# Linear attention and two expert layers on one core: scores masked on VectorE, scans one step earlier, state scaled on ScalarE, weight narrowing spread over three stages, sums of the second routing on TensorE

## The chip, the cores and the metric

The kernel runs on one core of a Trainium2 chip. Its engines are TensorE (PE; its weight loads are PEld), VectorE (DVE), ScalarE (ACT), GpSimd (POOL) and SyncE (SP, which here only issues transfers). Each engine works through its own instructions in order. The metric is the device time of one execution in microseconds; the kernel before takes 875.71 us (median of three runs, 875.18 to 875.74).

## The reference

Three parts follow one another. The first is linear attention with a decay, over 4 batches, 8 heads, 768 positions and a head size of 48. The second gives each of the 3072 tokens to one of 8 experts with room for 384 tokens each, in the order of the logits. The third is a dense layer with a squared ReLU.

```python
for t in range(S):
    state = alpha[:, :, t, :, None] * state + einsum('bhd,bhe->bhde', k[:, :, t], v[:, :, t])
    y[:, :, t] = einsum('bhd,bhde->bhe', q[:, :, t], state)
...
for idx in argsort(-logits.flatten()):
    tok, e = idx // E, idx % E
    if assigned[tok] >= 0 or counts[e] >= cap: continue
    assigned[tok] = e; counts[e] += 1
...
out[mask] = maximum(x[mask] @ w1[e], 0) @ w2[e]
...
g = maximum(x @ w_in, 0) ** 2
return g @ w_out
```

The two matrices of the last layer (384 x 2048 and 2048 x 384) come as 64-bit floats. The kernel reads their words as pairs of 32-bit integers and makes float32 of them ("narrowing"), kept as a high and a low half of 12 bits each.

## The kernel before

**Order.** The program order of each engine is the order in which the code is written; no scheduler moves anything. What is called first in the loop stands first in each engine's queue, and an instruction that waits holds up all behind it on its engine.

**Attention.** 24 chunks of 128 positions, 6 per batch, are the steps s = 0 to 23 of the main loop; two chunks are a unit (u = s // 2, c = s % 2). For each unit `prep` scales q and k: a VectorE scan over the alphas from behind (`f_t`, L144), GpSimd's product of k with it (L146), a reciprocal (L148), a copy of the ends (`be`, L149), a scan from ahead (`b_t`, L150) and the product of q with it (L152). `prep(u + 2)` runs a part at a time: the first scan at c = 1 of unit u, the second later in that step, the product of q at c = 0 of the next unit. In a step, `state_mm` (L231) makes the chunk's k v product, which VectorE adds to the state and multiplies by the decay (L239, L240); `scores` (L212) makes the scores of the next chunk, ScalarE copies them out of PSUM (L215) and GpSimd clears what lies above the diagonal (L216); `state_bd` (L248) copies the state into a block-diagonal tile; `k_tok` (L222) transposes k; `x_out` (L276 to L279) transposes the chunk before and writes it to DRAM (`x_d`); `y_mm` adds the part from the state (L256, full 128 x 128 products) and the part from the scores (L263); `logits` and `logits_t` make the router's logits, four chunks at a time.

**Narrowing.** `narrow` takes two pieces of 256 columns in every step: three VectorE instructions on each (L179, L182, L185), ScalarE's copy of the high half (L172) and GpSimd's difference (L173). The 48 raw pieces pass through four buffers; `narrow_load` issues the next transfer from SP as one comes free. All pieces are done about when the loop ends.

**First routing.** Six rounds find the threshold: products that count (L420), VectorE's test (`cg`), a product with a matrix of ones, VectorE's next digits, with warming products (L358) between. Then come the places, the chosen tokens' rows (L623, gathered by GpSimd) and the first expert's weights (`w_load0`, L798 and L799: high half on ScalarE, low half on VectorE).

**Experts.** For each of the 8 experts 8 steps of `gemm1` and `gemm2` and 16 of `gemm3` and `gemm4` run on TensorE. `tick` puts the next expert's routing between the products, a piece at a time: in each of 8 rounds `cross` issues two products (L428), three VectorE instructions (L433, L436, L437) and a GpSimd sum over all partitions (L440). VectorE reads that sum some products later.

Of the kernel before, what the change touches and what calls it, by code (L numbers as in the profile page):

```python
# [28 lines left out]
E = 8  # L29
# [13 lines left out]
NWP = 256  # L43
NWB = 4
BIG = 1.5e38
WD = 3
S0 = NS - 7
# [6 lines left out]
def kernel(ctx, tc, q, k, al, v, wg, w1, w2, w_in, w_out, out):  # L54
# [15 lines left out]
    wih = consts.tile([128, KD, F2], FR)  # L70
    wil = consts.tile([128, KD, F2], FR)
    woh = consts.tile([128, NF2, DM], FR)
    wol = consts.tile([128, NF2, DM], FR)

# [20 lines left out]
    def load(u, ends=(CU * HP,)):  # L95
        """q, k and alpha of a unit, whole or in parts of so many pairs"""
        i = u % NSL
        n0 = 0
        for n1 in ends:
            for t, src in ((as_[i], al), (ks[i].rearrange("p c a s -> p (c a s)"), k),  # L100
                           (qs[i].rearrange("p c a s -> p (c a s)"), q)):
# [15 lines left out]
    load(0, (2, 4, 8))  # L117
    load_v(0)
    bd = [ap_.tile([128, HP, 128], FT, name=f"bd{i}") for i in range(2)]
    nc.gpsimd.memset(bd[0], 0.0)  # L120
    nc.gpsimd.memset(bd[1], 0.0)
# [10 lines left out]
    def prep(u, n0=0, n1=CU * HP):  # L132
        """scaled q and k of one unit; yields after each VectorE scan"""
# [13 lines left out]
        yield  # L147
        nc.vector.reciprocal(d_b[:, cs, 0], f_t[:, cs, 0])  # L148
        nc.vector.tensor_copy(bend[i].rearrange("p c a -> p (c a)")[:, cs], f_t[:, cs, 0])  # L149
# [5 lines left out]
    wq = []  # L155
    for h_, l_, src in ((wih, wil, w_in), (woh, wol, w_out)):
        h2, l2, s2 = (t.rearrange("p a b -> p (a b)") for t in (h_, l_, src))
        wq += [(h2[:, j:j + NWP], l2[:, j:j + NWP], s2[:, j:j + NWP]) for j in range(0, h2.shape[1], NWP)]
    raws = []

    def narrow_load():
        if len(raws) < len(wq):
            raw = aw.tile([128, NWP, 2], U32, name="raw", bufs=NWB)
            nc.sync.dma_start(raw.rearrange("p a b -> p (a b)"), wq[len(raws)][2].bitcast(U32))
            raws.append(raw)

    def narrow():
        """float64 words -> float32 bits, kept as two halves of 12 bits each"""
        prev = []
        for i in range(0, len(wq) + 2, 2):  # L170
            for t, dst_h, dst_l in prev:
                nc.scalar.activation(dst_h, t.bitcast(FT), AF.Copy)  # L172
                nc.gpsimd.tensor_tensor(dst_l, t.bitcast(FT), dst_h.bitcast(FT), op=OP.subtract)  # L173
            prev = []
            if i < len(wq):
                js = (i, i + 1)
                ts = [aw.tile([128, NWP], U32, name=f"nb{j - i}") for j in js]
                for t, j in zip(ts, js):
                    nc.vector.tensor_scalar(t, raws[j][:, :, 1], 3, 0x3FFFFFF8, op0=OP.logical_shift_left,  # L179
                                            op1=OP.bitwise_and)  # L180
                for t, j in zip(ts, js):
                    nc.vector.scalar_tensor_tensor(t, raws[j][:, :, 1], 0xC0000000, t, op0=OP.bitwise_and,  # L182
                                                   op1=OP.bitwise_or)
# [531 lines left out]
    for _ in nw:  # L715
        pass
# [369 lines left out]
```

## Time and profile before

| what | value |
|---|---|
| median of three runs | 875.71 us |
| span of the profiled execution | 874.0 us |
| TensorE busy | 811.1 us (93%) |
| VectorE busy | 558.7 us (64%) |
| ScalarE busy | 398.1 us (46%) |
| GpSimd busy | 256.1 us (29%) |
| mean granted TensorE clock | 0.946 |
| chain that ended last | TensorE 69%, VectorE 16%, issue 10% |

The shares are means over stages with different limits. The attention lasts until about 192 us, the first routing until about 239 us, and the experts fill the rest. Rows of the timeline give the start and the length of an instruction, or of several alike (x8, say), whose lengths overlap a little; the distance between starts is what one takes of its engine.

### The profile page before, as it was taken

How to read it: one execution, taken by the hardware profiler on the slowest of the kernel's cores; microseconds unless marked ns; L12 is line 12 of the kernel's file. 1: busy time of each engine (PE TensorE's matmuls, PEld its weight loads, DVE VectorE, ACT ScalarE, POOL GpSimd, SP SyncE). 2: the span in 40 equal slices, each digit the busy share in tenths (PEclk: the TensorE clock that was granted, in tenths of full speed). 3: DMA queues.
4: the chain of work that ended last, by engine and by line, in shares of the span. 5: the costliest groups of instructions: out<-in, count | busy, mean ns of one | idle time of the engine just before them, and what ended most of it. 6: DMA issues, size and time to landing. Idle time of an engine off the chain costs nothing.

```text
span 874.0 us, 15157 instructions
## 1 busy us (share of the span) xinstructions
PE 811.1 (93%) x5592; PEld 764.8 (87%) x5592; DVE 558.7 (64%) x1528; ACT 398.1 (46%) x904; POOL 256.1 (29%) x248
## 2 busy tenths in 40 slices
PE   4876878789899999999999999999999999999996
PEld 3755767677599999999999999999999999999996
DVE  8999999983576577567656665765666542432211
ACT  3544546451234553464346245534634553662443
POOL 6687887960111131112201221220131210101001
PEclk9988787895799999999999999999999999999998
DMA  8557768521310230131023004201400332210000
GB/s 302 163 149 203 205 189 214 159 79 55 121 61 1 71 111 20 38 101 62 1 73 100 29 1 136 64 1 55 109 37 1 92 104 59 82 37 28 1 1 28
DMA packets 30219, 73.01 MB, mean 84 GB/s; under 512 B 4384, under 2 KB 8224, under 8 KB 30144
## 3 DMA queue, kind: packets, MB, share of 16 engines
q1 hardware_dynamic: 23616, 57.88, 23.2%
q0 software_dynamic: 3072, 9.44, 3.2%
q10 hardware_dynamic: 3456, 4.72, 1.6%
q8 instruction: 44, 0.72, 0.3%
q14 instruction: 31, 0.25, 0.1%
HBM read 62.58 MB, written 9.44 MB: 82 GB/s over the span
## 4 chain that ended last, share of the span: by engine, by line
PE 69%; DVE 16%; issue 10%; POOL 3%; DMA 2%; SPq 0%; ACT 0%; DVEq 0%; POOLq 0%; ACTq 0%
PE hu_p L842 10%; PE hu_p L844 10%; PE hu_p L843 10%; PE acc L926 7%; PE acc L927 7%; PE acc L922 7%; PE acc L842 3%; PE acc L844 3%; PE acc L843 3%; DVE nb L179 3%; DVE nb L182 3%; DVE nb L185 2%; DVE b_t L150 2%; DVE f_t L144 2%; PE rt_p L420 2%
## 5 line engine op out<-in xcount | busy, mean ns | idle before, releaser
L913 DVE TENSOR_TENSOR gl<-rg,gh 128x384 fp32r<-128x384 f32 x127 | 72.2, 568 | 165.5 <-ACT rg L912 164.7
L910 ACT ACTIVATE rg<-hu_p 128x384 f32<-128x384 f32 x128 | 63.0, 492 | 171.5 <-PE hu_p L844 168.1
L842 PE MATMUL hu_p<-zh,wih 128*128 128x384 f32 x384 | 131.5, 342 | 0.0
L926 PE MATMUL acc<-woh,gh 128*128 128x384 f32 x381 | 130.6, 343 | 0.0
L844 PE MATMUL hu_p<-zl,wih 128*128 128x384 f32 x384 | 129.9, 338 | 0.0
L843 PE MATMUL hu_p<-zh,wil 128*128 128x384 f32 x384 | 128.8, 335 | 0.0
L927 PE MATMUL acc<-wol,gh 128*128 128x384 f32 x381 | 128.6, 338 | 0.0
L440 POOL PARTITION_ALL_REDUCE tot<-ex x48 | 52.3, 1089 | 258.3 <-DVE ex L437 258.3
L922 PE MATMUL acc<-woh,gl 128*128 128x384 f32 x381 | 125.8, 337 | 0.0
L877 ACT ACTIVATE hh<-hu_p 128x384 fp32r<-128x384 f32 x64 | 31.5, 492 | 138.7 <-PE hu_p L844 138.7
L878 DVE SCALAR_TENSOR_TENSOR hl<-hu_p,hh 128x384 fp32r<-128x384 f32 x64 | 35.6, 556 | 63.9 <-ACT hh L877 63.8
L844 PEld LDWEIGHTS hu_p<-zl,wih 128*128 128x128 f32 x384 | 72.1, 188 | 1.2
L843 PEld LDWEIGHTS hu_p<-zh,wil 128*128 128x128 f32 x384 | 72.2, 188 | 0.0
L842 PEld LDWEIGHTS hu_p<-zh,wih 128*128 128x128 f32 x384 | 72.1, 188 | 0.0
L926 PEld LDWEIGHTS acc<-woh,gh 128*128 128x128 f32 x381 | 71.5, 188 | 0.1
L927 PEld LDWEIGHTS acc<-wol,gh 128*128 128x128 f32 x381 | 71.6, 188 | 0.0
L922 PEld LDWEIGHTS acc<-woh,gl 128*128 128x128 f32 x381 | 71.2, 188 | 0.0
L623 POOL DMA_INDIRECT xg<-x_d,ix x24 | 26.4, 1102 | 151.7 <-DVE pe L639 94.2
L911 ACT ACTIVATE gh<-rg 128x384 fp32r<-128x384 f32 x127 | 66.7, 525 | 4.0
L842 PE MATMUL hu_p<-xh,w1h 128*128 128x384 f32 x192 | 66.3, 345 | 0.0
L844 PE MATMUL hu_p<-xl,w1h 128*128 128x384 f32 x192 | 65.7, 342 | 0.0
L948 POOL DMA_INDIRECT out_dram<-ob,ix x24 | 23.7, 988 | 143.0 <-DVE ob L946 139.5
(252 smaller groups left out, 1885.6 us busy)
## 6 DMA issues: line engine op xcount, KB each, us to landing
wraw<-in_w_dram SPq DMA_DIRECT2D x62, 384.0 KB, 3.3
raw<-in_w_in_dram SPq DMA_DIRECT2D x24, 256.0 KB, 3.2
raw<-in_w_out_dram SPq DMA_DIRECT2D x24, 256.0 KB, 3.6
vt<-in_v_dram SPq DMA_DIRECT2D x12, 384.0 KB, 5.4
x_d<-xo ACTq DMA_DIRECT2D x24, 192.0 KB, 2.8
a<-in_al_dram SPq DMA_DIRECT2D x18, 193.7 KB, 4.7
k<-in_k_dram SPq DMA_DIRECT2D x18, 192.0 KB, 5.5
q<-in_q_dram SPq DMA_DIRECT2D x18, 192.0 KB, 6.1
```

The lines of the kernel that those rows point to most:

```text
L440: nc.gpsimd.partition_all_reduce(tot[:, :, :J], ex[:, :, :J], 128, bass_isa.ReduceOp.add)
L842: nc.tensor.matmul(dst, wh, xh, start=first, stop=False)
L843: nc.tensor.matmul(dst, wl, xh, start=False, stop=False)
L844: nc.tensor.matmul(dst, wh, xl, start=False, stop=last)
L877: nc.scalar.activation(hh, hp, AF.Relu)
L878: nc.vector.scalar_tensor_tensor(hl, hp, 0.0, hh.bitcast(FT), op0=OP.max, op1=OP.subtract)
L910: nc.scalar.activation(r, up, AF.Relu)
L911: nc.scalar.activation(gh, r, AF.Square)
L913: nc.vector.tensor_tensor(gl, g, gh.bitcast(FT), op=OP.subtract)
L922: nc.tensor.matmul(acc[j], gl[:, j * 128:(j + 1) * 128], woh[:, f, :], start=False, stop=(f == NF2 - 1))
L926: nc.tensor.matmul(acc[j], gh[:, cs], woh[:, f, :], start=(f == 0), stop=False)
L927: nc.tensor.matmul(acc[j], gh[:, cs], wol[:, f, :], start=False, stop=False)
```

## The change

- **Masking.** The scores go from PSUM to SBUF by one VectorE instruction for each half, a bitwise AND with a mask of ones and zeros. ScalarE's copies and GpSimd's clearing are gone.
- **State.** VectorE still adds; the decay is four ScalarE instructions with a scale per partition. The block-diagonal tile is gone: the part of y from the state is eight products of 48 x 48 blocks in place of four of 128 x 128, into two PSUM tiles, one for each half, and ScalarE copies them out in two instructions in place of one.
- **Scans.** `prep(u + 2)` begins at c = 0: first scan at c = 0, second scan and product of q at c = 1. The alphas are loaded a unit further ahead, k at the end of c = 0, q at the end of c = 1. `prep(1)` runs whole before the loop. The copy of the ends goes to ScalarE.
- **Narrowing.** 16 pieces of 768 columns, each a slice of 128 of both matrices. Raw words lie in 16 tiles of their own and are overwritten by their halves. One of the three VectorE instructions of a piece runs in every second step (four pieces in the attention), twelve more follow one by one through the first routing (four more pieces), and the other eight pieces, cut in two of 384 columns, in the first expert: one instruction kind in each of the 8 steps of `gemm1`, two in each step of `gemm4`.
- **First expert's weights.** Of the 8 low halves the first three stay on VectorE, five go to GpSimd.
- **Second routing.** For expert 1 alone the sum over all partitions is a product with a matrix of ones, issued right behind the two products of `cross`.
- **Logits.** Two chunks at a time, and the last two chunks by token.

```diff
     def scores(s):
...
         for r in range(2):
             t = aw.tile([128, HP, 128], FT, name=f"am{r}")
-            nc.scalar.activation(t, sc_p[r], AF.Copy)
-            nc.gpsimd.affine_select(t, t, [[0, HP], [1, C]], OP.is_ge, 0.0, base=0, channel_multiplier=-1)
+            nc.vector.tensor_tensor(t.bitcast(I32), sc_p[r].bitcast(I32),
+                                    mask[:, None, :].to_broadcast([128, HP, 128]), op=OP.bitwise_and)
...
-        sc = bend[j][R, cn, :, None].to_broadcast([64 + D, HP, D])
+        src = st_p[R, :, :D]
         if s % NC:
             t0 = aw.tile([128, HP, D], FT, name="st0", bufs=1)
-            nc.vector.tensor_tensor(t0[R], st_p[R, :, :D], st[s - 1][R], op=OP.add)
-            nc.vector.tensor_tensor(t[R], t0[R], sc, op=OP.mult)
-        else:
-            nc.vector.tensor_tensor(t[R], st_p[R, :, :D], sc, op=OP.mult)
+            nc.vector.tensor_tensor(t0[R], src, st[s - 1][R], op=OP.add)
+            src = t0[R]
+        for p in range(HP):
+            nc.scalar.activation(t[R, p, :], src[:, p, :], AF.Copy, scale=bend[j][R, cn, p:p + 1])
...
             for p in range(HP):
-                nc.tensor.matmul(y_p[:, p, :], bd[s % 2][:, p, :], qs[i][:, c, p, :],
-                                 start=(p == 0), stop=False, skip_group_check=True)
+                for r in range(2):
+                    rr = slice(64 * r, 64 * r + D)
+                    nc.tensor.matmul(y_p[r][rr, p, :], st[s - 1][rr, p, :], qs[i][rr, c, p, :],
+                                     start=(p == 0), stop=False, skip_group_check=True)
...
+        for f in range(NF2):
+            raw = raws[f, 0]
+            if fine[0] is None:
+                ps = [(aw.tile([128, NWP], U32, name="nb"), slice(0, NWP))]
+            else:
+                ps = [(fine[0].tile([128, DM], U32, name="nb", tag="ob", bufs=3), slice(i * DM, (i + 1) * DM))
+                      for i in range(2)]
+            for t, cs in ps:
+                nc.vector.tensor_scalar(t, raw[:, cs, 1], 3, 0x3FFFFFF8, op0=OP.logical_shift_left,
+                                        op1=OP.bitwise_and)
+            yield False
+            for t, cs in ps:
+                nc.vector.scalar_tensor_tensor(t, raw[:, cs, 1], 0xC0000000, t, op0=OP.bitwise_and,
+                                               op1=OP.bitwise_or)
+            yield False
+            for t, cs in ps:
+                nc.vector.scalar_tensor_tensor(t, raw[:, cs, 0], 29, t, op0=OP.logical_shift_right,
+                                               op1=OP.bitwise_or)
+            w = consts.tile([128, 2, NWP], FR, name=f"w{f}", tag=f"w{f}")
+            for t, cs in ps:
+                nc.scalar.activation(w[:, 0, cs], t.bitcast(FT), AF.Copy)
+            for t, cs in ps:
+                nc.gpsimd.tensor_tensor(w[:, 1, cs], t.bitcast(FT), w[:, 0, cs].bitcast(FT), op=OP.subtract)
...
+            if pe:
+                tot = rt_p[:, 200:200 + E * J].rearrange("p (e j) -> p e j", e=E)
+                nc.tensor.matmul(tot, ones, ex[:, :, :J], start=True, stop=True)
+                return tot
...
-        if c == 1:
+        if c == 0:
             pr = prep(u + 2) if u + 2 < NU else iter(())
...
-        if s + 2 < NS:
-            next(nw, None)
         if c == 1:
             next(pr, None)
+        elif s < 2 * NA_:
+            next(nw)
         y_mm(s)
...
-        if c == CU - 1 and u + NSL < NU:
-            load(u + NSL)
-        if c == CU - 1 and u + 2 < NU:
-            load_v(u + 2)
+        if c == 0:
+            load(u + NSL, "k")
+        else:
+            load(u + NSL, "q")
+            load(u + NSL + 1, "a")
+            if u + 2 < NU:
+                load_v(u + 2)
+        narrow_load()
...
-            nc.vector.tensor_tensor(fl, got[n], fh.bitcast(FT), op=OP.subtract)
+            (nc.vector if n < 3 else nc.gpsimd).tensor_tensor(fl, got[n], fh.bitcast(FT), op=OP.subtract)
```

The first place is VectorE's queue in the middle of the attention. Before, one step from the first scan (`f_t`) to the next step's add of the state (`st`), with six narrowing instructions (`nb`):

```order
L144 SCALAR_TENSOR_TENSOR f_t<-a_95,d_f 128x1032
L179 TENSOR_SCALAR nb_1782<-raw 128x256
L179 TENSOR_SCALAR nb_1783<-raw 128x256
L182 SCALAR_TENSOR_TENSOR nb_1782<-raw,nb_1782 128x256
L182 SCALAR_TENSOR_TENSOR nb_1783<-raw,nb_1783 128x256
L185 SCALAR_TENSOR_TENSOR nb_1782<-raw,nb_1782 128x256
L185 SCALAR_TENSOR_TENSOR nb_1783<-raw,nb_1783 128x256
L148 RECIPROCAL d_b<-f_t 128x8
L149 COPY be_98<-f_t 128x8
L150 SCALAR_TENSOR_TENSOR b_t<-a_95,d_b 128x1032
L239 TENSOR_TENSOR st_1825<-st_p,st 112x192
```

After, the same stretch and the rest of a whole unit (`am` are the masked scores, `L` the logits):

```order
L144 SCALAR_TENSOR_TENSOR f_t<-a_83,d_f 128x1032
L231 TENSOR_TENSOR am_1216<-rt_p,mask 128x512
L231 TENSOR_TENSOR am_1218<-sc_p_127,mask 128x512
L188 SCALAR_TENSOR_TENSOR nb<-raw_402,nb 128x768
L255 TENSOR_TENSOR st_1275<-st_p,st 112x192
L149 RECIPROCAL d_b<-f_t 128x8
L150 SCALAR_TENSOR_TENSOR b_t<-a_83,d_b 128x1032
L231 TENSOR_TENSOR am_1292<-rt_p,mask 128x512
L231 TENSOR_TENSOR am_1294<-sc_p_127,mask 128x512
L152 TENSOR_TENSOR q_85<-q_85,b_t 128x1024
L309 TENSOR_REDUCE L<-lg_p 128x16
L255 TENSOR_TENSOR st_1347<-st_p,st 112x192
```

The twelve narrowing instructions of a unit have become one, three times as wide, and four masking instructions have come in behind the scans.

The second place is TensorE's queue in the first expert, at the first round of the second routing. Before, the two products of `cross` (`rt_p`) stand between those of the expert:

```order
L844 MATMUL hu_p_2412<-xl,w1h 128x384
L428 LDWEIGHTS oh
L428 MATMUL rt_p<-m,oh 96x180
L428 LDWEIGHTS oh
L428 MATMUL rt_p<-m,oh 96x180
L842 MATMUL hu_p_2412<-xh,w1h 128x384
```

After, a third product follows them at once; it waits for VectorE (`ex`), and the expert's products stand behind it:

```order
L869 MATMUL acc_2182<-hl,w2h 128x384
L441 LDWEIGHTS oh
L441 MATMUL rt_p<-m,oh 96x180
L441 LDWEIGHTS oh
L441 MATMUL rt_p<-m,oh 96x180
L454 LDWEIGHTS ones
L454 MATMUL rt_p<-ex,ones 128x120 [waits DVE_49]
L867 MATMUL acc_2183<-hh,w2h 128x384
```

The third place is VectorE's queue after the change in that expert, at the second round (`eq`, `cn` and `ex` lead to the product with ones, `hl` is the low half of the expert's hidden layer):

```order
L427 TENSOR_TENSOR m<-xn,jc 128x360 [waits DVE_49]
L184 TENSOR_SCALAR nb<-raw_1410 128x384
L184 TENSOR_SCALAR nb<-raw_1410 128x384 [waits Pool_49]
L446 TENSOR_TENSOR eq<-rt_p,own 96x180 [waits PE_49]
L449 TENSOR_REDUCE cn<-eq 96x15 [waits DVE_49]
L450 TENSOR_TENSOR ex<-cn,same 96x8x15 [waits DVE_49]
L903 SCALAR_TENSOR_TENSOR hl<-hu_p_2180,hh 128x384 [waits Activation_49]
L188 SCALAR_TENSOR_TENSOR nb<-raw_1410,nb 128x384 x2
```

Two narrowing instructions stand ahead of the three that the product with ones waits for, and the second of them waits for GpSimd.

## Rows read from the trace of the kernel before

**Rows 1.** Windows: stretch, length, busy PE PEld DVE ACT POOL, clock, DMA share, GB/s

```profile
60.00:80.00 20.00, 15.19 (x199) 12.63 (x199) 19.96 (x26) 9.20 (x21) 17.36 (x14) 0.83 0.59 162
185.00:195.00 10.00, 10.00 (x126) 8.63 (x122) 8.95 (x26) 5.42 (x13) 5.84 (x6) 1.00 0.15 48
240.00:290.00 50.00, 49.63 (x282) 48.88 (x281) 33.16 (x107) 19.10 (x37) 9.30 (x8) 0.96 0.08 31
```

**Rows 2.** Timeline of VectorE: three scans of the attention

```profile
13.24 2.31 DVE L144 TENSOR_TENSOR_SCAN f_t<-a,d_f 128x1032 f32<-128x1032 f32 x1
...
41.14 2.30 DVE L144 TENSOR_TENSOR_SCAN f_t<-a,d_f 128x1032 f32<-128x1032 f32 x1
...
165.00 2.29 DVE L144 TENSOR_TENSOR_SCAN f_t<-a,d_f 128x1032 f32<-128x1032 f32 x1
```

**Rows 3.** Groups of VectorE instructions by line, first 200 us

```profile
L179 DVE TENSOR_SCALAR nb<-raw 128x256 uint32<-128x256 uint32 x48 | 34.2, 751 | 3.6 <-POOL wil L173 2.3 <-POOL wol L173 1.2
L185 DVE SCALAR_TENSOR_TENSOR nb<-raw,nb 128x256 uint32<-128x256 uint32 x48 | 28.7, 638 | 0.0
...
L182 DVE SCALAR_TENSOR_TENSOR nb<-raw,nb 128x256 uint32<-128x256 uint32 x48 | 28.3, 630 | 0.0
```

**Rows 4.** Timeline of TensorE, steps 22 and 23 of the attention

```profile
184.75 0.56 PE L231 MATMUL st_p<-vt,kt 128*48 128x48 f32 x16
...
186.34 0.60 PE L222 MATMUL kt_p<-ident,k 112*128 112x112 f32 x4
186.78 1.07 PE L256 MATMUL y_p<-q,bd 128*128 128x128 f32 x8
...
189.12 1.16 PE L256 MATMUL st_p<-q,bd 128*128 128x128 f32 x8
...
191.56 0.49 PE L295 MATMUL lt_p<-ident,lg 104*128 104x104 f32 x3
```

**Rows 5.** Timeline of VectorE, part of one unit

```profile
143.51 2.29 DVE L150 TENSOR_TENSOR_SCAN b_t<-a,d_b 128x1032 f32<-128x1032 f32 x1
145.73 0.32 DVE L239 TENSOR_TENSOR st<-st_p,st 112x192 f32<-112x192 f32 x1
146.09 0.36 DVE L240 TENSOR_TENSOR st<-st,be 112x192 f32<-112x192 f32 x1
146.37 1.22 DVE L152 TENSOR_TENSOR q<-q,b_t 128x1024 f32<-128x1024 f32 x1
147.50 0.48 DVE L179 TENSOR_SCALAR nb<-raw 128x256 uint32<-128x256 uint32 x2
147.91 0.75 DVE L182 SCALAR_TENSOR_TENSOR nb<-raw,nb 128x256 uint32<-128x256 uint32 x2
148.58 0.75 DVE L185 SCALAR_TENSOR_TENSOR nb<-raw,nb 128x256 uint32<-128x256 uint32 x2
```

**Rows 6.** Groups of the page: busy us, mean ns of one

```profile
L878 DVE SCALAR_TENSOR_TENSOR hl<-hu_p,hh 128x384 fp32r<-128x384 f32 x64 | 35.6, 556 | 63.9 <-ACT hh L877 63.8
```

**Rows 7.** Timelines of GpSimd and VectorE, at 21 us and at 141 us

```profile
20.83 2.20 POOL L146 TENSOR_TENSOR k<-k,f_t 128x1024 f32<-128x1024 f32 x1
...
20.93 2.72 DVE L182 SCALAR_TENSOR_TENSOR nb<-raw,nb 128x256 uint32<-128x256 uint32 x2
...
141.03 1.76 POOL L173 TENSOR_TENSOR wol<-nb,woh 128x256 fp32r<-128x256 f32 x2
```

**Rows 8.** Timeline of VectorE, last round of the first routing

```profile
222.20 0.15 DVE L495 TENSOR_SCALAR cg<-rt_p 32x8 f16<-32x8 f32 x1 [2.63 <-PE rt_p L420]
223.07 0.17 DVE L509 TENSOR_REDUCE dp<-rt_p 128x1 f32<-128x8 f32 x1 [0.71 <-PE rt_p L497]
```

**Rows 9.** Timelines of TensorE and VectorE, first round of the second routing

```profile
248.81 0.32 PE L428 MATMUL rt_p<-m,oh 128*96 128x180 f16 x2
249.74 0.34 DVE L433 TENSOR_TENSOR eq<-rt_p,own 96x180 f16<-96x180 f32 x1
...
250.56 0.28 DVE L437 TENSOR_TENSOR ex<-cn,same 96x120 f16<-96x120 f16 x1
```

More of the change, by code (lines that the diff above doesn't have):

```diff
@@ L115, in load_v @@
         nc.sync.dma_start(vs[u], v[u])
-    load(0, (2, 4, 8))
+    load(0, ends=(2, 4, 8))
     load_v(0)
-    bd = [ap_.tile([128, HP, 128], FT, name=f"bd{i}") for i in range(2)]
-    nc.gpsimd.memset(bd[0], 0.0)
-    nc.gpsimd.memset(bd[1], 0.0)
+    mask = ap_.tile([128, 128], I32, name="mask")
+    yts = [ap_.tile([128, HP, 128], FT, name=f"yt{i}") for i in range(NYT)]
+    for t in yts:
+        nc.gpsimd.memset(t, 0.0)
     d_f = ap_.tile([128, CU * HP, W], FT, name="d_f")
@@ L153, in prep @@
         yield
[L155 to L165, printed above, removed]
@@ new lines, with narrow_load @@
+    raws, wi, wo = {}, {}, {}
+    def narrow_load(n=1):
+        for _ in range(n):
+            f, o = divmod(len(raws), 2)
+            if f >= NF2:
+                return
+            if not o:
+                raw = consts.tile([128, NWP, 2], U32, name=f"raw{f}", tag=f"w{f}")
+                nc.sync.dma_start(raw[:, :DM].rearrange("p (a b) t -> p a (b t)", a=KD),
+                                  w_in[:, :, f * 128:(f + 1) * 128].bitcast(U32))
+            else:
+                raw = raws[f, 0]
+                nc.sync.dma_start(raw[:, DM:].rearrange("p a t -> p (a t)"), w_out[:, f, :].bitcast(U32))
+            raws[f, o] = raw
@@ L191, with narrow_upto @@
+    def narrow_upto(n):
+        while len(wo) < n:
+            next(nw)
     sc_p = [rt_p.rearrange("p (a b) -> p a b", a=HP), pp.tile([128, HP, 128], FT, name="sc_p1")]
-    y_p = pp.tile([128, HP, 128], FT, name="y_p")
+    y_p = [pp.tile([128, HP, 128], FT, name=f"y_p{r}") for r in range(2)]
     kt_p = pp.tile([128, HP, 128], FT, name="kt_p")
@@ L268, in y_mm @@
         else:
-            yt[s] = aw.tile([128, HP, 128], FT, name="yt")
-        for ps in ([slice(0, HP)] if s < NS - 1 else [slice(0, HP // 2), slice(HP // 2, HP)]):
-            nc.scalar.activation(yt[s][:, ps], y_p[:, ps], AF.Copy)
+            yt[s] = yts[s % NYT]
+        for r in range(2):
+            rr = slice(64 * r, 64 * r + D)
+            nc.scalar.activation(yt[s][rr], y_p[r][rr], AF.Copy)
     def x_out(s):
@@ L421, in count, with cross @@
                                  stop=(c == NS - 1))
[L423 removed]
+        def cross(self, i, pe):
             J = self.J[i]
@@ L499, in routing @@
                 else:
-                    cp = key.cross(i)
+                    cp = key.cross(i, kk == 1)
                     yield TA
@@ L660 @@
     NE = NS - 4
-    pr = prep(1)
-    next(pr)
-    next(pr)
+    load(3, "a")
+    for _ in prep(1):
+        pass
     for s in range(NS):
@@ L673 @@
             scores(s + 1)
-        if not last:
-            state_bd(s)
-        if s + 1 < NS:
+        if s + 1 < NS and (s + 1) % NC != NC - 1:
             k_tok(s + 1)
@@ L712 @@
     key0.ahead(1, key0.x)
+    narrow_load(2 * NF2)
     r0 = routing(0)
     next(r0)
-    for _ in nw:
-        pass
+    at = next(nw)
     for _ in range(len(WIDE) - 1):
@@ L719 @@
         x_out(next(late))
+        at = next(nw)
         next(r0)
+        at = next(nw)
+    while not at:
+        at = next(nw)
     att.close()
```

127 lines of the change are left out of this document (56 added, 71 removed).

## The prediction

> **What bounds the kernel now.** I read the windows first. From 60 to 80 us VectorE is busy 19.96 of 20 us, TensorE 15.19 at a granted clock of 0.83, ScalarE 9.20; in the experts TensorE is busy 49.63 of 50 us [rows 1]. So the attention goes at VectorE's pace and the experts at TensorE's, and a gain must come from the first and survive the second. The starts of the first scan give the pace: from unit 3's at 41.14 to unit 11's at 165.00 lie eight units of 15.5 us [rows 2]. The groups by line say what fills them: narrowing took 34.2 + 28.7 + 28.3 = 91 us of VectorE in the first 200 us [rows 3], over half as wide again as the scans. [...]
>
> GpSimd makes VectorE's part worse. While GpSimd's product of k ran (20.83, for 2.20), two narrowing instructions took 2.72 that take 0.75 with GpSimd idle [rows 5, 7]. That is why L182 has a mean of 630 ns against 335 from start to start in the quiet pair [rows 3, 5].
>
> **The attention after the change.** VectorE, per unit: scan 2.2, scan 2.2, product of q 1.13, two adds of the state 0.36 each [rows 5]. Four maskings of 512 columns: the low half from PSUM with 384 columns takes 0.556 [rows 6]; in proportion that is 0.74, and by the 1.13 of 1024 columns of q [rows 5] 0.57; I take 0.69, nearer to the row that reads PSUM: 2.8. One narrowing instruction of 768 columns: three times 0.335, so 1.0, or three times 0.205 for the first kind (147.50 to 147.91 for two) [rows 5], mean 0.87. For the reciprocal and the sum of the logits I allow 0.4, one add. Sum 10.3.
>
> The scan frees k, so GpSimd's 2.20 [rows 7] starts with the maskings (1.4) and the narrowing behind them finds it still running: 0.9 more. So **11.2 per unit** against 15.5. If VectorE met nothing, 10.3; if it also waited elsewhere, at the maskings and where a low half runs (below), 12.6.
>
> [...]
>
> TensorE, per unit at the full clock: 4.37 a step without the transposes of the output, which are four like k's (0.44, 186.34 to 186.78), and 0.1 for the logits' transposes. The state's part of y becomes 16 passes on 48 x 48 blocks in place of 8 (1.07) [rows 4]; two blocks lie in different rows and columns of the array, as the two scores of a pair lie in different rows, and those 16 passes fit between the state's end (185.31) and 186.34, 1.0 us [rows 4]. So 5.0 a step and **10.1 a unit**; without pairing twice the 1.07, 12.2 a unit. TensorE stays just below VectorE and waits in short pieces, so I expect the full clock.
>
> The rest is no limit: ScalarE loses four copies of 512 columns and four small ones and gains smaller ones, from 9.20 of 20 us; GpSimd keeps 2.2 of its work a unit and a low half every third. Transfers: 0.59 of the engines' time at 162 GB/s [rows 1] are 2.5 MB in 15.5 us; a unit now brings 0.79 MB of raw weights in place of 1.05, 2.25 MB in 11.2 us, 200 GB/s, share 0.73. q is issued a step, an add, a scan and two maskings before its product, some 9 us.
>
> **The sum to the end of the attention.** At the start four maskings (2.8), and the scores of chunk 1 between them since they need the bank back (1.0, twice that at the low clock), come ahead of unit 1's scan: from 13.24 to 17.6 [rows 2, 4]. Then unit 1 whole (5.7), unit 2's scan 2.2, narrowing with its wait 1.8, two adds, reciprocal and the rest of unit 2 (5.6): unit 3's scan at 33 against 41.14. Eight units of 11.2, the routing's constants (2) and three low halves that meet a product of q (1 each) bring unit 11's scan to 127.6 against 165.00. From there 10.7 (the rest of steps 18 and 19), three steps of 5.0 on TensorE and step 23 with 2.44 (189.12 to 191.56) end the products of y at 156 against 191.56 [rows 2, 4]. **Gain 35.6.** Bounds: at TensorE's 10.1 a unit and without the low halves' 3, 47; at 12.6 a unit, 24.
>
> **The first routing: 2 lost** (1.3 to 5). Most of its narrowing lies under products that count, where VectorE waits (2.63 before `cg`). In the last round, though, two instructions of 768 stand between `cg` and `dp` (1.0 each): 222.20 + 0.15 + 2.0 is 224.35, against 223.07 [rows 8]. The last low half on GpSimd may hold a small product behind that: 0.7. At worst that happens in each of the four pieces.
>
> **The first expert: 16 lost** (9 to 36). Two things. First, TensorE's order: the product with ones stands right behind those of `cross`, so TensorE stops until `eq`, `cn` and `ex` are through. Before, the products ended at 249.13 and `ex` at 250.84, 1.7 later, since VectorE was busy; the three alone take 1.1 (249.74 to 250.84) [rows 9]. Eight rounds of 1.5: 12, between 9 and 14. GpSimd's sum, which it replaces, was not in TensorE's way. Second, VectorE: 33.2 of 50 us before [rows 1]; five low halves leave (about 1 each, twice L878's 384 columns [rows 6]), and 48 narrowing instructions of 384 columns come: 16 of 0.3 and 32 of 0.5 (half as much again as 0.205 and 0.335), 21 in all [rows 5]. That is 49 of 50. Beside it GpSimd gets five differences of 768 and sixteen of 384 at 0.88 for 256 [rows 7]: 34 us. The stops stretch the 50 us to 62, which gives VectorE room again; I take 4 more for queueing.
>
> **Sum.** 874.0 - 35.6 + 2 + 16 = 856.4 for the span. The median of the three runs is 1.7 above the span; **858**.
>
> **Rivals.**
> *The port and the queue in the first expert give it all back.* VectorE's narrowing (21) and its other products with two SBUF inputs (some 10 of the 33) cannot run beside GpSimd's 34: 65 us in a stretch that was 50. The stops add 12. Where a narrowing instruction that waits for GpSimd stands ahead of `eq` (the third excerpt), a stop grows by a difference of 768, 2.6; four of them add 10. That makes 37 in place of 16: 874.0 - 35.6 + 2 + 37 + 1.7 = 879. It decides against the change once the first expert costs over 33.6. Against it: a difference on GpSimd and a stop of TensorE can overlap, and hl and eq read PSUM. [...]
> *TensorE becomes the bound of the attention.* VectorE meets nothing, 47 gained; the stops are at 1.1: 874.0 - 47 + 1.3 + 9 + 1.7 = 839. For it: the full-clock step; against it: the collision with k's product has a row.
> *Waiting in the attention.* VectorE is held more, q's transfer is late, or the blocks don't pair (12.2): 12.6 a unit, 24 gained: 874.0 - 24 + 2 + 16 + 1.7 = 870. A granted clock that stays at 0.83 would make TensorE's unit 12.2, which is inside this.
> *It moves the narrowing and no more.* Its columns are the same, and half of them still stand where time counts. If the queue of the first expert takes what the attention saved, this is the first rival.
>
> **How the numbers follow.** Forecast (849 to 867) 0.55; TensorE-bound attention (below 849) 0.18; waiting attention (867 to 874) 0.10; between 874 and 877.4 0.04; the first rival 0.13. A measurement of this kernel can tell about 0.2%, 1.75 us, from no change. So faster 0.83, same 0.04, slower 0.13. The range that leaves out two in ten: 838 to 878; below it lies about a tenth, above it most of the first rival.
>
> **What would show it.** Right: unit 11's scan near 128 and 11.2 between scans; TensorE at the full clock and over 85% busy in the attention; the end of y near 156; eight TensorE waits on `ex` of 1.1 to 1.7 in the second routing; expert 1's first product 16 later than the shift of the attention says. Wrong: scans 10 or 12.6 apart; a granted clock below 0.9 in the attention; waits on `ex` of 3 or more, or VectorE waiting on GpSimd for narrowing buffers; TensorE waiting for low halves in the second layer of the first expert.

## The result and the profile after

The changed kernel took 884.09 us (median of four, 880.81 to 888.95), the kernel before 875.73 beside it (875.18 to 875.94): ratio 1.0103, 95% interval 1.0070 to 1.0135. It is slower, by about 1%. The forecast was 858, with a range that ended at 878.

The profiled execution is the longest of the four (span 887.2 against 874.0). Three marks cut it into stages: the end of the last products of y, the first product of the first expert, and the first product of the second expert.

| stage | before | after | difference | forecast |
|---|---|---|---|---|
| start to the end of y | 191.6 | 162.1 | -29.5 | -35.6 |
| first routing, to the first expert's first product | 47.4 | 49.8 | +2.4 | +2 |
| first expert, to the second expert's first product | 80.2 | 120.5 | +40.3 | +16 |
| the rest | 554.7 | 554.8 | +0.1 | 0 |

So the attention gave most of what was forecast, and the first expert cost 24 more than was forecast. Over the whole span GpSimd has a third less to do than before (256.1 us), and TensorE is busy longer (811.1):

```profile
PE 816.5 (92%) x5743; PEld 764.7 (86%) x5743; DVE 548.6 (62%) x1471; ACT 389.4 (44%) x909; POOL 169.5 (19%) x175
```

These are the windows after, as in [rows 1], and under them those of the first expert, of the kernel after and of the one before (columns: stretch, length, busy PE, PEld, DVE, ACT, POOL, clock, DMA share, GB/s):

```profile
60.00:80.00 20.00, 19.34 (x310) 15.76 (x309) 19.41 (x22) 13.79 (x38) 4.37 (x2) 0.99 0.79 231
140.00:150.00 10.00, 9.85 (x162) 7.87 (x158) 8.26 (x13) 6.10 (x18) 0.02 (x1) 1.00 0.68 217
212.00:332.00 120.00, 91.39 (x465) 87.36 (x466) 79.28 (x229) 43.11 (x94) 28.42 (x24) 0.87 0.13 41
```

```profile
239.00:319.00 80.00, 79.63 (x459) 78.16 (x459) 52.65 (x186) 36.49 (x80) 12.47 (x12) 0.97 0.19 61
```

Between 60 and 80 us TensorE is now busy 19.34 of 20 us at the full clock (0.99), where it had 15.19 at 0.83. That holds for this stretch and not for the whole attention; the next three of 20 us have a lower clock:

```profile
80.00:100.00 20.00, 19.00 (x260) 15.83 (x262) 19.18 (x21) 10.26 (x27) 7.48 (x3) 0.83 0.82 212
100.00:120.00 20.00, 14.97 (x190) 12.43 (x186) 13.55 (x15) 8.15 (x24) 2.18 (x1) 0.74 0.81 220
120.00:140.00 20.00, 17.77 (x251) 14.11 (x246) 17.34 (x18) 10.18 (x24) 7.45 (x3) 0.83 0.80 226
```

In the first expert TensorE needed 79.63 us of 80 before. After, nearly the same products (465 records against 459; the eight products with ones are new) keep it busy for 91.39 us, since it runs part of the time at a granted clock of 0.50 (from 269.88 to 275.50 us, for one), and 28.6 us are idle: 11.8 + 28.2 are the 40. What TensorE waited for from 205 to 365 us (us in total, times, longest):

```profile
PE rt_p L454 <- DVE ex L450: 18.5, 8, 5.6
PE acc L869 <- DVE hl L903: 4.2, 1, 4.2
PE rt_p L441 <- DVE m L427: 3.8, 3, 3.0
```

The first row is the product with ones: eight stops of 2.3 on the mean, where 1.5 was forecast. One of them, as a timeline of VectorE, TensorE and GpSimd (start, length):

```profile
266.08 1.02 DVE L188 SCALAR_TENSOR_TENSOR nb<-raw,nb 128x384 uint32<-128x384 uint32 x2
267.01 1.02 DVE L192 SCALAR_TENSOR_TENSOR nb<-raw,nb 128x384 uint32<-128x384 uint32 x2
267.95 0.33 DVE L446 TENSOR_TENSOR eq<-rt_p,own 96x180 f16<-96x180 f32 x1
268.32 0.34 DVE L449 TENSOR_REDUCE cn<-eq 96x15 f16<-96x180 f16 x1
268.67 2.03 POOL L198 TENSOR_TENSOR w<-nb,w 128x384 fp32r<-128x384 f32 x2 [4.46 <-ACT w L196]
268.69 1.13 DVE L450 TENSOR_TENSOR ex<-cn,same 96x120 f16<-96x120 f16 x1
269.88 0.26 PE L454 MATMUL rt_p<-ex,ones 128*128 128x120 f16 x1 [3.82 <-DVE ex L450]
269.90 0.67 PE L867 MATMUL hu_p<-zh,w 128*128 128x384 f32 x1
270.37 0.52 PE L868 MATMUL hu_p<-zh,w 128*128 128x384 f32 x1
...
275.17 0.52 PE L868 MATMUL hu_p<-zh,w 128*128 128x384 f32 x1
275.49 0.39 PE L869 MATMUL hu_p<-zl,w 128*128 128x384 f32 x1
275.72 0.33 PE L867 MATMUL hu_p<-zh,w 128*128 128x384 f32 x1
275.88 0.33 PE L868 MATMUL hu_p<-zh,w 128*128 128x384 f32 x1
```

The products of `cross` were through at 266.06. Four narrowing instructions stood ahead of `eq` in VectorE's queue: 1.9 us. Then `ex`, which takes 0.28 in [rows 9], took 1.13: GpSimd's difference had started 0.02 before it, and `ex` ended about 0.1 after the first of the two differences in that row. TensorE stopped for 3.82 and afterwards ran at the low clock (0.50 granted) for 5.6 us, 0.32 between starts in place of 0.17. All three losses are in these rows.

### The profile page after: what moved, and what is told of

It reads as the page before. It is cut to its first block, busy times and chain, and to the rows that moved or that the text cites. A ratio compares the mean times of both kernels' runs of the same rounds, so it can differ in the third digit from the quotient of the medians.

```text
span 887.2 us, 15226 instructions
## 1 busy us (share of the span) xinstructions
PE 816.5 (92%) x5743; PEld 764.7 (86%) x5743; DVE 548.6 (62%) x1471; ACT 389.4 (44%) x909; POOL 169.5 (19%) x175
## 4 chain that ended last, share of the span: by engine, by line
PE 63%; issue 9%; DVE 6%; POOL 1%; ACT 1%; DMA 0%; POOLq 0%; ACTq 0%; DVEq 0%
PE hu_p L867 10%; PE hu_p L869 10%; PE hu_p L868 10%; PE acc L951 6%; PE acc L952 6%; PE acc L947 6%; PE acc L867 3%; PE acc L869 3%; PE acc L868 3%; PE rt_p L433 2%; PE y_p L371 1%; PE rt_p L441 1%; PE xq_p L860 1%; DVE nb L192 1%; POOL out_dram L973 1%
## 5 line engine op out<-in xcount | busy, mean ns | idle before, releaser
L951 PE MATMUL acc<-w,gh 128*128 128x384 f32 x381 | 132.5, 348 | 0.6 <-ACT gh L936 0.6
L867 PE MATMUL hu_p<-zh,w 128*128 128x384 f32 x384 | 132.8, 346 | 0.0
L869 PE MATMUL hu_p<-zl,w 128*128 128x384 f32 x384 | 130.9, 341 | 0.0
L952 PE MATMUL acc<-w,gh 128*128 128x384 f32 x381 | 130.2, 342 | 0.0
L868 PE MATMUL hu_p<-zh,w 128*128 128x384 f32 x384 | 129.9, 338 | 0.0
L947 PE MATMUL acc<-w,gl 128*128 128x384 f32 x381 | 127.3, 341 | 0.5 <-DVE gl L938 0.5
L951 PEld LDWEIGHTS acc<-w,gh 128*128 128x128 f32 x381 | 72.7, 191 | 9.7 <-issue 7.1
L867 PEld LDWEIGHTS hu_p<-zh,w 128*128 128x128 f32 x384 | 73.1, 190 | 4.0 <-issue 4.0
L869 PEld LDWEIGHTS hu_p<-zl,w 128*128 128x128 f32 x384 | 73.0, 190 | 1.2
L947 PEld LDWEIGHTS acc<-w,gl 128*128 128x128 f32 x381 | 72.5, 191 | 0.9 <-DVE gl L938 0.8
L868 PEld LDWEIGHTS hu_p<-zh,w 128*128 128x128 f32 x384 | 73.2, 191 | 0.0
L952 PEld LDWEIGHTS acc<-w,gh 128*128 128x128 f32 x381 | 72.8, 191 | 0.0
L869 PE MATMUL acc<-hl,w2h 128*128 128x384 f32 x192 | 65.7, 342 | 4.2 <-DVE hl L903 4.2
L867 PE MATMUL acc<-hh,w2h 128*128 128x384 f32 x192 | 66.3, 345 | 0.0
```

Of the source, the lines that this page charges most:

```text
L867: nc.tensor.matmul(dst, wh, xh, start=first, stop=False)
L868: nc.tensor.matmul(dst, wl, xh, start=False, stop=False)
L869: nc.tensor.matmul(dst, wh, xl, start=False, stop=last)
L947: nc.tensor.matmul(acc[j], gl[:, j * 128:(j + 1) * 128], wo[f][:, 0, :], start=False, stop=(f == NF2 - 1))
L951: nc.tensor.matmul(acc[j], gh[:, cs], wo[f][:, 0, :], start=(f == 0), stop=False)
L952: nc.tensor.matmul(acc[j], gh[:, cs], wo[f][:, 1, :], start=False, stop=False)
```

## Experiments

Each kernel is the changed one with the edit shown, unless another is named. All times are medians, against a kernel before at 875.6 to 876.3. The single times of one kernel spread by 2 to 9.5 us, so a difference of two medians is uncertain by some 2 to 5. Part of the spread comes from the attention, whose end lies anywhere from 154.7 to 162.1 us in the traces with the same attention. Where it matters, the length of the first expert in the one trace of each run stands beside the median, by the marks of the table above.

**Three parts of the first expert, taken back one at a time and together.**

```diff
-                    cp = key.cross(i, kk == 1)
+                    cp = key.cross(i, False)
```

> The changed kernel, with the sums of the second routing back on GpSimd (all else as changed). In its trace TensorE's first expert has 28.6 us of waiting and 12.3 us more of busy time at a lower clock than before; 18.5 of the waiting stand at the product with ones. My theory (that product is the larger half of the loss): these 18.5 go, and with them two thirds of the 12.3, so 884 - 26 = 858, waits on `ex` gone. Rival one (VectorE's queue, full of narrowing, is the limit): the stop only moves on to `m` and `hl`, and GpSimd has eight sums more; at most 9 gained, 875 or above.

Measured: 918.96, ratio 1.0502 (1.0469 to 1.0534). 35 slower than with the product with ones. The theory falls. The number of rival one (875 or above) holds and the stops did move to `m` (37.2 in five), but nothing in it makes the kernel slower than it was. Without the product with ones something worse comes up (below), so this run can't say what that product costs.

```diff
-            (nc.vector if n < 3 else nc.gpsimd).tensor_tensor(fl, got[n], fh.bitcast(FT), op=OP.subtract)
+            nc.vector.tensor_tensor(fl, got[n], fh.bitcast(FT), op=OP.subtract)
```

> The changed kernel, with all eight low halves of the first expert's weights on VectorE as before. My theory: GpSimd's five differences are a small part; VectorE takes five instructions of about 1 us more and is held five times less: between 880 and 887. Rival (the port is the larger part): each of the five differences of 1.8 us holds a small VectorE instruction ahead of the product with ones, so that a stop and the low clock after it go: some 12 gained, 872.

Measured: 877.34, ratio 1.0029 (1.0006 to 1.0053). 6.8 gained, between the two. The port, in the first rival, here and in later expectations, stands for this alone: a VectorE instruction that takes longer beside one of GpSimd. The rows for it are under the first rival below. The stops at the product with ones stay (19.5); the stop of 4.2 on `hl` is gone. In the traces the first expert goes from 120.5 to 117.7, so only 2.8 shorter.

```diff
             raw = raws[f, 0]
+            if f >= NF2 // 2:
+                wi[f], wo[f] = wi[f - NF2 // 2], wo[f - NF2 // 2]
+                continue
```

> The changed kernel without the narrowing in the first expert: the last eight pieces are left out and the halves of the first eight are used a second time (the raw words are still loaded). My theory: the eight stops at the product with ones shrink from 18.5 to the 12 of the forecast, the waits on `hl` (4.2) and `m` (3.8) go, and half of the 12.3 of low clock: 20 gained, 864. Rival one (VectorE's queue is the whole loss): 35 gained, 849. Other rival (the product with ones costs the same whatever stands beside it): 8 gained, 876.

Measured: 859.66, ratio 0.9818 (0.9798 to 0.9838). 24 gained; the stops at ones shrink to 10.1, and the mean granted clock of the profiled execution is 0.955, where the changed kernel's is 0.944. The wait on `hl` stays (3.6).

> All three edits at once: sums on GpSimd, low halves on VectorE, no narrowing in the first expert (its last eight pieces are left out, the first eight's halves used twice). Every theory that names these three expects the first expert at the 112 us that it took before and 884 - 40 = 844; a time well above that would say that something else in the change costs there.

Measured: 843.15, ratio 0.9630 (0.9611 to 0.9649). The first expert takes 79.4, against 80.2 before by the marks of the table (the 112 of the expectation is not this stage). The stages ahead of it are those of the changed kernel, and they give 33.1 here (876.25 - 843.15) against the forecast's 35.6 - 2 = 33.6. Nothing outside the three parts costs anything in that expert.

**One part alone.** The product with ones (the two other edits together), then the narrowing (the first two edits together):

> The product with ones by itself: as changed, but low halves on VectorE and no narrowing in the first expert (its last eight pieces are left out, the first eight's halves used twice). The kernel without all three took 843.2. Theory (each stop is the run of three VectorE instructions, 1.1 to 1.5, and the clock drops little): eight stops of 1.3, 843 + 10 = 853. Rival (with VectorE free the stops vanish under the product before, and all cost is made by the narrowing): 845 or below. Rival (each stop brings a stretch at the low clock): 860 or above.

Measured: 855.94, ratio 0.9778 (0.9760 to 0.9797): 12.7 more than without all three. Eight stops of 10.8 in all, the longest 1.9:

```profile
PE rt_p L457 <- DVE ex L453: 10.8, 8, 1.9
```

> The narrowing by itself in the first expert: as changed, but sums of the second routing on GpSimd and low halves on VectorE. With low halves on GpSimd too this took 919.0, with none of the three 843.2. Theory now (a ring through the queues: VectorE's next narrowing instruction waits for a GpSimd difference, that one stands behind a GpSimd sum, which waits for a VectorE instruction behind the narrowing): most of the 76 stays, 890 to 915, and VectorE waits for GpSimd's differences and sums. Rival (the five low halves in GpSimd's queue make it): below 870.

Measured: 911.85, ratio 1.0421 (1.0400 to 1.0442): 68.7 more than without all three. GpSimd's timeline in that run, first part of the first expert:

```profile
228.79 1.96 POOL L198 TENSOR_TENSOR w<-nb,w 128x384 fp32r<-128x384 f32 x2 [7.20 <-issue]
236.54 1.04 POOL L457 PARTITION_ALL_REDUCE tot<-ex  x1 [5.79 <-issue]
244.34 2.00 POOL L198 TENSOR_TENSOR w<-nb,w 128x384 fp32r<-128x384 f32 x2 [6.76 <-issue]
252.13 1.04 POOL L457 PARTITION_ALL_REDUCE tot<-ex  x1 [5.79 <-issue]
256.76 1.65 POOL L457 PARTITION_ALL_REDUCE tot<-ex  x1 [3.59 <-DVE ex L450]
```

Whenever GpSimd goes from a sum over all partitions to a difference or back in that expert it stands idle for 5.8 to 7.2 us, in nine of the eleven changes with nothing in the trace to wait for; in the run with the low halves on GpSimd too (918.96) twelve changes show 5.8 to 7.5. Between two sums, or two differences, it waits for its inputs alone. What GpSimd does in these gaps is not shown. The next kernel takes the changes away: the sixteen differences of that expert go to VectorE.

```diff
-                nc.gpsimd.tensor_tensor(w[:, 1, cs], t.bitcast(FT), w[:, 0, cs].bitcast(FT), op=OP.subtract)
+                (nc.vector if fine[0] else nc.gpsimd).tensor_tensor(w[:, 1, cs], t.bitcast(FT), w[:, 0, cs].bitcast(FT), op=OP.subtract)
```

> The narrowing by itself again (sums of the second routing on GpSimd, low halves on VectorE: 911.9, against 843.2 without narrowing there), but with the sixteen differences of the first expert on VectorE in place of GpSimd. In the trace of the 911.9 GpSimd stands idle for 5.7 to 7.2 us each time that it goes from a sum over all partitions to a difference or back, and not between two of a kind. Theory (this changeover, ten to eleven times, is the 69 us): without differences GpSimd does nothing but sums there, the gaps go, and there remain VectorE's 14 for narrowing and up to 9 for sixteen differences of 0.55: 857 to 870. Rival (the ring of waits through the narrowing buffers, which this also shortens but which keeps ScalarE): 885 or above.

Measured: 865.47, ratio 0.9895 (0.9862 to 0.9928), inside what the theory said; every gap between its sums is a wait for `ex`. So 46 of the 69 go with the changes of kind (911.85 - 865.47), although VectorE has sixteen differences more; the other 22 stay with VectorE's narrowing and differences. The same edit shortens the ring of waits through the buffers; what that alone gives was not measured.

**Where the product with ones stands.**

```diff
-                nc.tensor.matmul(tot, ones, ex[:, :, :J], start=True, stop=True)
                 return tot
...
                     cp = key.cross(i, kk == 1)
-                    yield TA
+                    if kk == 1:
+                        yield 4
+                        nc.tensor.matmul(cp, ones, ex[:, :, :J], start=True, stop=True)
+                        yield TA - 4
+                    else:
+                        yield TA
```

> As changed, but the product with ones is issued four steps of the interleaving later (12 products of the expert, 2.1 us at the full clock), the digits after it one step behind. Theory (the place of that product makes the stops): of 18.5 us of stops some 4 stay, those longer than 2.1, and with them goes most of the low clock: 884 - 22 = 862. Rival (VectorE's queue is late for everything, the stops move to `m` and `hl`): 876 or above.

Measured: 866.93, ratio 0.9899 (0.9861 to 0.9937): 17.2 gained by issuing that product, and the digits behind it, later. Four stops of 7.5 in all are left at ones, 4.2 at `hl`, 2.9 at `m`.

**What makes the narrowing cost 21 beside the product with ones (877.3 against 855.9).** First the wait for GpSimd's difference ahead of `eq`, which the third excerpt of the change shows. Half by half the same instructions use the three buffers singly:

```diff
+                for o in range(2):
+                    raw = raws[f, o]
+                    t = fine[0].tile([128, DM], U32, name="nb", tag="ob", bufs=3)
...
             if kk == 0:
                 next(wl[0], None)
                 next(nw, None)
+                next(nw, None)
```

> As changed, but the narrowing in the first expert goes half by half (384 columns through all three instruction kinds, then the next 384; same instructions, same number in each step), so that the three buffers turn over singly and VectorE need not wait for the GpSimd difference of the piece just done. Theory (that wait stands ahead of `eq`, `cn`, `ex` and makes the stops at the product with ones longer than VectorE's three instructions): VectorE's waits for GpSimd's differences go, the stops shrink from 18.5 to 12, the low clock by half: 884 - 13 = 871. Rival (the stops come from VectorE's own load and the port, not from that wait): 880 to 887.

Measured: 884.14, ratio 1.0088 (1.0064 to 1.0113), the same as the changed kernel. VectorE's waits for the difference (4.3 us) are gone from the trace, and the stops at ones are 19.5. The theory falls: nothing is gained by taking that wait away.

Then each half of the narrowing by itself, with low halves on VectorE:

> Product with ones as changed, low halves of the expert's weights on VectorE, and of the narrowing in the first expert only VectorE's and ScalarE's instructions: the sixteen GpSimd differences are left out (the low halves of the first eight pieces are used a second time). With them 877.3, without any narrowing there 855.9. Theory (VectorE's own 48 instructions, in front of those that TensorE waits for, are the 21 us): 872 to 877. Rival (the port: GpSimd's differences hold VectorE): 864 or below.

Measured: 870.01, ratio 0.9947 (0.9924 to 0.9969): 14.1 above 855.9.

> The opposite half: VectorE's 48 narrowing instructions in the first expert are left out, ScalarE's copies and GpSimd's differences stay (they work on the first eight pieces' high halves). Theory (VectorE's queue): 855 to 860. Rival (the port): 866 or above. If both halves are small and only the two together make 21, the cause is how they meet: VectorE's two-input narrowing held by GpSimd's difference.

Measured: 861.78, ratio 0.9839 (0.9804 to 0.9873): 5.9 above 855.9. The two add up to 20.0 of 21.4. In the traces the first expert takes 91.7 without narrowing, 107.3 with VectorE's part, 97.7 with GpSimd's and 117.7 with both: 15.6 and 6.0 of 26.0. So VectorE's own queue is the larger part and GpSimd's differences the smaller; whether some 4 us come only when both are there, these runs can't tell. ScalarE's copies are in both halves.

**Versions.** The first has low halves on VectorE, the product with ones four steps later, and in the second layer one narrowing instruction kind a step in place of two. The second has low halves on VectorE, the later product, and the narrowing half by half. The third is the second with `load_v` ahead of the load of alpha in the attention; the fourth is the second with three and two half instructions a step in turn in the second layer in place of four.

> The product with ones four steps later, all low halves on VectorE, and the narrowing in the second layer one instruction kind a step in place of two. Theory: three causes of queueing at the product with ones are gone, the first expert costs 5 to 15 more than its 80 to the next expert's first product: 850 to 858, faster than both kernels. Rival (the nb buffers, three for pairs, still hold VectorE until GpSimd is through, and TensorE stops on hl or gl): 865 or above.

Measured: 878.98, ratio 1.0046 (1.0030 to 1.0062). What the denser pace delivered in time now comes too late: TensorE waits 14.5 us for the halves themselves (us in total, times, longest).

```profile
PE hu_p L872 <- POOL w L198: 8.3, 2, 7.9
PE hu_p L871 <- ACT w L196: 6.2, 2, 5.5
PE rt_p L519 <- DVE ex L450: 5.8, 5, 2.1
```

> Narrowing half by half in the first expert, the product with ones four steps later, and all low halves of the first expert's weights on VectorE. The product four steps later alone gave 866.9. Theory: the remaining stops there (7.5 at ones, 4.2 at hl, 2.9 at m) came from the wait for GpSimd and from the low halves on GpSimd, so 853 to 859. Rival (VectorE's load decides what is left): 864 or above.

Measured: 863.80, ratio 0.9863 (0.9843 to 0.9882), just at the rival's border, and the lowest median of the versions that do all of the work: 1.4% below the kernel before. Its interval overlaps those of the later product alone (866.93) and of sums on GpSimd with that expert's differences on VectorE (865.47).

> As the run before, and in the attention v of the unit after next is loaded ahead of alpha instead of behind it. Theory: the waits of the state's products for v, 0.5 to 6.7 us from one execution to the next, go and nothing takes their place: 1 to 3 less than the run before, and a narrower spread. Rival (alpha or the raw words come late instead): the same or more.

Measured: 872.43, ratio 0.9962 (0.9940 to 0.9985). The rival holds: the waits for v grew (10.6 in four) and GpSimd's product of k waited 46.8 us for k, in five waits:

```profile
POOL k L146 <- DMA k<-in_k_dram: 46.8, 5, 10.6
```

In the changed kernel that row has 4.8 in one. Which transfer holds up which was not taken further.

> As the run with halves, the later product and low halves on VectorE (863.8), but the narrowing in the second layer goes at three and two half instructions a step in turn, in place of four. Theory (VectorE is overfull for some 45 us: 17.8 of 20 us busy, while the second half of that layer has room): the stops in these steps shrink, 856 to 861. Rival (the halves now come too late and TensorE waits for them, as in the run with one instruction a step): 866 or above.

Measured: 867.43, ratio 0.9916 (0.9891 to 0.9941), slower than the four a step. TensorE does not wait for halves, so the rival's mechanism is not it either. In its trace the stops at ones did shrink, from 8.7 in the 863.8 to 5.1, but TensorE was busy for 87.18 us in the first expert in place of 83.35, at a granted clock of 0.94 in place of 0.98. Why the clock is lower with fewer stops stays open.

## Why the prediction was wrong

**The attention: right in its sum, in part by errors that cancel.** With the first expert's three parts taken back the stages ahead of it gain 33.1, and 33.6 was forecast. The units are uneven, though. In the profiled execution two are 11.25 and 11.15 us apart (forecast 11.2), the eight from unit 3 to unit 11 take 12.5 on the mean. In the fourteen other traces with the same attention (three of them load the raw words in smaller pieces) single units take 10.4 to 13.9 and the eight 92 to 96 together, where the forecast has 94.6 with the constants and the low halves; unit 3 starts at 35.0 to 35.9 in place of 33. Nor did TensorE have the full clock: 0.89 to 0.94 in those traces, from 40 us to ten before the end of y, while it was busy for 88 to 93%. That sign was named as wrong for a clock below 0.9; it came up in stretches, and the sum came out all the same. One of the two units, from VectorE's timeline after, answers to [rows 2, 5]:

```profile
82.26 2.30 DVE L144 TENSOR_TENSOR_SCAN f_t<-a,d_f 128x1032 f32<-128x1032 f32 x1
84.48 0.66 DVE L231 TENSOR_TENSOR am<-rt_p,mask 128x512 int32<-128x512 int32 x1
85.06 0.68 DVE L231 TENSOR_TENSOR am<-sc_p,mask 128x512 int32<-128x512 int32 x1
85.66 2.02 DVE L192 SCALAR_TENSOR_TENSOR nb<-raw,nb 128x768 uint32<-128x768 uint32 x1
...
91.23 1.61 DVE L152 TENSOR_TENSOR q<-q,b_t 128x1024 f32<-128x1024 f32 x1
93.31 0.23 DVE L309 TENSOR_REDUCE L<-lg_p 128x16 f32<-128x64 f32 x1 [0.47 <-PE lg_p L308]
93.51 2.31 DVE L144 TENSOR_TENSOR_SCAN f_t<-a,d_f 128x1032 f32<-128x1032 f32 x1
```

The 11.2 took it that GpSimd's product of k does not hold the maskings; no row of the kernel before shows a masking, so that was the author's assumption. Here one takes 0.66 to 0.68 (0.69 was taken), also while that product runs (84.69 for 2.17), so the wait at the maskings that the 12.6 allowed for did not come. The narrowing behind them is held until that product ends (2.02, 1.8 was taken; 0.93 to 0.96 with GpSimd idle). TensorE's steps are 5.16 and 4.70 (y at 141.86, 147.02, 151.72; 5.0 was taken, from the 4.37 between 184.75 and 189.12 in [rows 4]), and the 16 passes of the state's blocks take 1.0 (140.85 to 141.86), no more than the 1.07 of the eight in [rows 4]: they do pair. The end of y at 156 was missed only in this one execution, where the products of the state waited 6.7 us for v. The fourteen other traces end it between 154.7 and 158.3 us. Here are the first scan of unit 11 and the last products of y in the run without all three parts (127.6 and 156 were forecast):

```profile
128.29 2.31 DVE L144 TENSOR_TENSOR_SCAN f_t<-a,d_f 128x1032 f32<-128x1032 f32 x1 [0.23 <-issue]
```

```profile
153.93 1.47 PE L278 MATMUL y_p<-am,vt 128*48 128x128 f32 x16
```

TensorE did not become the bound of the attention, and the waiting attention came up in the profiled execution alone (12.5 a unit, 29.5 gained). The late v (waits of 0.5 to 6.7 us in all, by the traces with the same loads) had no term.

**The first routing: right.** 2.4 in the profile after, 3.2 in the run without all three; 2 with a range of 1.3 to 5. So was the mechanism: in the last round two narrowing instructions stand between `cg` and `dp`, which start 1.93 apart in place of 0.87, and GpSimd's last difference holds a small instruction behind them, for 1.6 us where 0.7 was taken (`sa` took 0.18 before):

```profile
197.24 1.81 POOL L198 TENSOR_TENSOR w<-nb,w 128x768 fp32r<-128x768 f32 x1 [3.38 <-ACT w L196]
```

```profile
197.31 1.79 DVE L583 TENSOR_TENSOR sa<-abh 128x24 f32<-128x24 f16 x1
```

**The first expert: the step that failed.** The term was "12 for the product with ones, 4 more for queueing". By the runs:

| | by the medians, us | first expert, one trace each, us |
|---|---|---|
| product with ones alone | 12.7 (855.9 - 843.2) | 12.3 (91.7 - 79.4) |
| narrowing beside it | 21.4 (877.3 - 855.9) | 26.0 (117.7 - 91.7) |
| five low halves on GpSimd on top | 6.8 (884.1 - 877.3) | 2.8 (120.5 - 117.7) |
| together | 40.9 | 41.1 |

The 12 was right within a microsecond, and its mechanism too: eight stops, 10.8 us. The "4 more for queueing" measured 28.2. The mis-step was the sentence that VectorE would have 49 us of work in a stretch of 62 and so have room. VectorE did have room, although its busy time rose by 26.6 (from 52.65 to 79.28) where 21 - 5 was counted: in none of the six stretches of 20 us that make up the 120 is it busy for more than 15.03. But TensorE's stops aren't set by VectorE's mean load. They are set by what stands ahead of three small instructions at the moment of the round, and four narrowing instructions are 1.9 us there, more than the three themselves. Each stop was then priced without what follows it, the low clock: TensorE's busy time rose by 11.8 us for the same products. In the run with the product with ones alone, where no stop is longer than 1.9, TensorE was busy for 81.20 us in that stretch at a clock of 0.98, so nearly the 79.63 of before:

```profile
206.00:298.00 92.00, 81.20 (x471) 78.77 (x470) 52.18 (x187) 36.92 (x80) 3.87 (x4) 0.98 0.17 52
```

**The first rival** (0.13 of the chance) came near, with 37 and 879 where 40.9 and 884.1 were measured, but in part by luck. Its 12 for the stops measured 12.7. Its 10 for narrowing that waits for GpSimd ahead of `eq` measured nothing. No run shows its 15 for VectorE held beside GpSimd, the port (65 us in a stretch of 50); at most 12.7 answers to it: 6.8 for the low halves on GpSimd and 5.9 for GpSimd's differences, 2.8 and 6.0 by the traces. Nor does a row of the kernel before show a product other than narrowing held; that was the author's assumption. In the trace after VectorE is held, though. Three narrowing instructions of 384 columns that started beside a difference took 1.14 to 1.17, and 0.35 without one. The two `kb` on 24 columns, the first with a single input, took 0.18 and 0.17 in the kernel before and 1.81 and 1.82 here, and `m` behind them 1.94 for 0.34; `eq` between the two, with two inputs in SBUF, kept its 0.35:

```profile
215.15 1.81 DVE L404 TENSOR_SCALAR kb<-vm 128x24 int32<-128x24 int32 x1
216.88 0.35 DVE L406 TENSOR_TENSOR eq<-L,vm 128x192 f32<-128x192 f32 x1
217.15 1.82 DVE L407 TENSOR_TENSOR kb<-kb,vm 128x24 int32<-128x24 int32 x1
...
219.93 1.94 DVE L427 TENSOR_TENSOR m<-x,jc 128x360 f16<-128x360 f16 x1
```

```profile
215.09 1.84 POOL L824 TENSOR_TENSOR w2l<-rg,w2h 128x768 fp32r<-128x768 f32 x1 [5.84 <-ACT w2h L823]
216.88 2.04 POOL L824 TENSOR_TENSOR w1l<-rg,w1h 128x768 fp32r<-128x768 f32 x1
219.75 1.92 POOL L824 TENSOR_TENSOR w2l<-wraw,w2h 128x768 fp32r<-128x768 f32 x1 [0.83 <-ACT w2h L823]
```

Both `kb` end when GpSimd's difference ends, and `m` 0.2 after the next. The `hl` behind them starts at 222.33, and TensorE's stop of 4.2 on it is the one that goes with the low halves back on VectorE. The 14.1 of VectorE's own queue had no price in any case of the prediction.

**What would have set it right.** The third excerpt of the change showed two narrowing instructions ahead of `eq`. The prediction let a stop grow there only in the first rival, for four rounds, and by the wait for GpSimd and not by the two instructions themselves. Had each of the eight stops been given the two or four instructions ahead of it (1 to 1.9 us), the stops alone would have been 20 to 27, where 18.5 were measured at that product and 8.0 at `hl` and `m`. With the 11.8 of low clock that followed, which only the trace after shows, that makes 32 to 39, around the 33.6 from which the change loses. Also, "GpSimd's sum was not in TensorE's way" was true of the kernel before and wrong of this one: with the narrowing in that expert the sum on GpSimd costs 35 more than the product with ones (918.96 against 884.09).

## What to carry to other kernels

Work that is moved "beside" a stage that another engine bounds cost, in this kernel, mostly what it put ahead of the few instructions that the bounding engine waits for, and not what it added to a mean load. So count the queue at each such wait. A product that depends on a chain of another engine should be issued some products later than its inputs are asked for: four steps later gave back 17 of 41 us here. And keep one engine to one kind of instruction within a stage if a change of kind has a gap in the trace (5.8 to 7.5 us each on GpSimd here).

## What the runs showed of the hardware

- In two runs GpSimd stood idle for 5.8 to 7.5 us in each of 23 changes from a sum over all partitions to an elementwise difference or back; no instruction stands in the trace for it.
- A VectorE instruction on 24 columns took 1.81 us beside a GpSimd difference of 1.84 that had started 0.06 earlier, and 0.18 in the kernel before. The masking of 512 columns, which reads its scores from PSUM, took 0.66 to 0.68 beside GpSimd.
- After a stop of 3.82 us TensorE's products stood 0.32 apart, at a granted clock of 0.50, for 5.6 us before they were 0.17 apart again. With eight stops of 1.35 on the mean the granted clock over the first expert stayed at 0.98.
